# Moving four Q blocks behind the K/V loop, a minimum from GpSimd to VectorE, LN2 statistics from VectorE to ScalarE, and new PSUM banks in a fused attention and FFN kernel

## The chip, the cores and the metric

The kernel runs on one core of one Trainium2 chip. The metric is device time in microseconds (us), the median of several executions. The profile of the core shows a matrix engine (PE), VectorE (DVE), ScalarE (ACT), GpSimd (POOL) and a queue engine (SP) that issues DMAs. In its traces each works through its own list of instructions in order and waits for the others. The program puts its matmuls into eight PSUM banks, 512 columns at most in each, and lets PE use a bank again only when DVE or ACT has read it out.

All runs quoted are marked fast in the record. Two timings of one kernel still differ by up to 0.5% (868.22 to 872.25 us in the runs of before), and part of this document finds out why.

## The reference, cut to what matters

```python
mod = silu(c) @ w_mod                          # six vectors: sa, ca, ga, sb, cb, gb
h = layernorm(x) * (1 + ca) + sa               # x: 2048 tokens x 1024
q, k, v = split(h @ wqkv)                      # 32 heads of 32
pq, pk = phi(q), phi(k)                        # phi(t) = (t > 0 ? t + 1 : exp(t)) + 1e-6
kv = sum over tokens of pk^T v                 # one 32x32 matrix a head
z = sum over tokens of pk
o = (pq @ kv) / (pq . z + 1e-6)
x = x + ga * (o @ wo)
h = layernorm(x) * (1 + cb) + sb               # LN2
x = x + gb * ((gelu(h @ w_gate) * (h @ w_up)) @ w_down)
```

`phi` is computed as min(exp(t), 1) + 1e-6 plus max(t, 0): one ACT pass (exp), one DVE or POOL pass (min), one DVE pass (max and add).

## The kernel before

The tokens are 16 chunks of 128, and four chunks make a token group of 512. The stages are these.

1. **K/V loop.** For each chunk, K and V (four blocks of eight matmuls), `kvacc` (the sum kv, one chunk late), and two Q blocks of the group before. A Q block is eight matmuls of 512 columns for 128 of the 1024 Q columns of one group.
2. **Unit stage.** The Q blocks of the last group, the denominators (`den`), the transposes of kv (`kvt`), eight products kv·Wo (`w2_pair`), and the scaling of pq by 1/den (`bcast`: small matmuls that spread 1/den over the partitions, then DVE multiplications `pqs`).
3. **Wo stage.** Twelve of the sixteen chunks of o·Wo with the residual addition on DVE, LN2 of group 0, the scaling of groups 2 and 3.
4. **FFN** for the four groups, each with `up` and `gate` products and then `down`. The last four Wo chunks lie between products of the first group.

A small scheduler in the program records each operation with what it reads and writes and sets the waits. So the order in the source is the order on each engine. The parts that matter:

```python
def phi(bank, dst_ap, dst_rng, note, min_eng=V):
    ...exp on ACT...
    o = sch.op(min_eng, lambda e: e.tensor_scalar(EB[i], EB[i], 1.0, 1e-6, op0=ALU.min, op1=ALU.add), ...)
    ...max and add on DVE...

def q_evac(sg, qc, b):                       # the last four Q blocks: minimum on POOL
    phi(b, PQ[sg][:, qc, :], ..., G if sg == NSG - 1 and qc >= 4 else V)

for c_ in range(4, NCH):                     # K/V loop
    if c_ % 4 == 0:
        q_todo += [(c_ // 4 - 1, qc) for qc in range(NG)]
    for _ in range(2):
        q_block(*q_todo.pop(0))
    ...K, V, kvacc(c_ - 1), LN1 of chunk c_ + 3...
    if c_ == 13:                             # POOL: iota and four is_equal passes make SEL
        ...
    if c_ >= 12:                             # DVE: Wo *= ga, two rows of blocks a chunk
        ...

# unit stage
q_block(3, 0, False, 0); kvacc(15); zcols(); q_evac(3, 0, 0)
q_block(3, 1, bank=1);   kvbd();    q_block(3, 2, bank=2);  den(0, 5); kvt()
q_block(3, 3, bank=0);   w2_pair(0)
q_block(3, 4, bank=1);   bcast(0, 0); w2_pair(1)
q_block(3, 5, bank=0);   w2_pair(2);  bcast(0, 1); w2_pair(3)
q_block(3, 6, bank=1);   w2_pair(4);  bcast(0, 2); w2_pair(5)
q_block(3, 7, bank=0);   w2_pair(6);  bcast(0, 3); w2_pair(7)

# Wo stage
for c_ in range(12):
    wo_chunk(c_, 2 * (c_ % 2))               # banks 0/1 or 2/3
    if c_ == 1: den(1, 4)
    if 3 <= c_ < 7: bcast(1, c_ - 3)
    if 5 <= c_ < 9: ln2_a(c_ - 5, False)     # statistics on DVE, x-hat on ACT, transpose by DMA
    if c_ == 9: mod2(0, 2)                   # DVE: scale and shift of h
    if c_ == 10: mod2(2, 2)
```

Of the kernel before, what the change touches and what calls it, by code (L numbers as in the profile page):

```python
# [7 lines left out]
ACTF = mybir.ActivationFunctionType  # L8
# [4 lines left out]
D = 1024  # L13
NCH = S // P
NSG = 4
# [201 lines left out]
def bass_adaLN_cond__linear_attn_block__geglu_ffn__prompt_kernel(  # L217
# [14 lines left out]
    with ExitStack() as es:  # L232
# [96 lines left out]
        def r_pq(sg, k0=0, k1=NG, s0=0, s1=SGW):  # L329
            return r_t8(PQO[sg], f"pq{sg}", k0, k1, s0, s1)  # L330
# [240 lines left out]
        KVB = {g: (5 + g // 3, (g % 3) * KV_SLOT) for g in range(NG)}  # L571
        eb_i = [0]

        def phi(bank, dst_ap, dst_rng, note, min_eng=V):
            i = eb_i[0] % 6
            eb_i[0] += 1
            rng = r_2k(EBO[i], f"eb{i}")
            sch.op(A, lambda e: e.activation(EB[i][:, :], PS(bank), ACTF.Exp), prd=pr(bank), wr=rng, note=f"{note}.exp")
            o = sch.op(min_eng, lambda e: e.tensor_scalar(EB[i][:, :], EB[i][:, :], 1.0, 1e-6, op0=ALU.min, op1=ALU.add),
                       rd=rng, wr=rng, deps=[last_g[0]] if min_eng == G else [], note=f"{note}.min")  # L580
            if min_eng == G:
                last_g[0] = o
            sch.op(V, lambda e: e.scalar_tensor_tensor(dst_ap, PS(bank), 0.0, EB[i][:, :], op0=ALU.max, op1=ALU.add),
                   rd=rng, prd=pr(bank), wr=dst_rng, note=f"{note}.add")

# [42 lines left out]
        def q_block(sg, qc, evac=True, bank=None):  # L628
            b = nb() if bank is None else bank
            o = None  # L630
            for dc in range(NDC):
                o = sch.op(T, lambda e, dc=dc: e.matmul(PS(b), WQ[:, dc, qc * P:(qc + 1) * P], H1[sg][:, dc, :],  # L632
                                                        start=(dc == 0), stop=(dc == NDC - 1)),
                           rd=r_w(OFF_WQ, "wq", dc, qc * P, (qc + 1) * P) + r_h1(sg, dc, dc + 1),
                           pwr=(pr(b) if dc == 0 else ()), note=f"q sg{sg} qc{qc} dc{dc}")
            pset_writer(b, o)
            if evac:
                q_evac(sg, qc, b)
            return b

        def q_evac(sg, qc, b):
            phi(b, PQ[sg][:, qc, :], r_pq(sg, qc, qc + 1), f"phiq{sg}.{qc}", G if sg == NSG - 1 and qc >= 4 else V)


        for c_ in range(3):
# [52 lines left out]
        for c_ in range(4, NCH):  # L698
            if c_ % 4 == 0:
                q_todo += [(c_ // 4 - 1, qc) for qc in range(NG)]  # L700
            for _ in range(2):
                q_block(*q_todo.pop(0))
            for jg in range(2):
                b = nb()
                kv_mm(c_, "k", jg, b, list(range(NDC)))
                k_evac(c_, jg, b)
            for jg in range(2):
                b = nb()
                kv_mm(c_, "v", jg, b, list(range(NDC)))
                v_evac(c_, jg, b)  # L710
            if c_ % 2 == 1 and c_ + 2 < NCH:
                mod1(c_ + 1, 2)
            kvacc(c_ - 1)
            if c_ + 3 < NCH:
                ln1(c_ + 3)
                t1d(c_ + 3)
            if c_ == 6:
                o_r = mod_rows(0, 4)
                for k, t in enumerate((6, 7, 8, 9)):
                    wm_dma(t, k)  # L720
                sch.dma(Q, lambda e: e.dma_start(GAB[:, :].rearrange("p (a b) -> p a b", a=2),
                                                 scr_row[0, 0:2, :].rearrange("(o a) b -> o a b", o=1).to_broadcast([P, 2, 512])),
                        wr=R_GAB, deps=[o_r], note="gab")
                sch.dma(Q, lambda e: e.dma_start(GBB[:, :].rearrange("p (a b) -> p a b", a=2),
                                                 scr_row[0, 2:4, :].rearrange("(o a) b -> o a b", o=1).to_broadcast([P, 2, 512])),
                        wr=R_GBB, deps=[o_r], note="gbb")
            if c_ == 9:
                o_r = mod_rows(1, 4)
                sch.dma(Q, lambda e: e.dma_start(SBT[:, :], scr_row[1, 0:2, :].rearrange("a (b p) -> p (a b)", p=P)),
                        wr=r_sm("sbT"), deps=[o_r], note="sbT")  # L730
                sch.dma(Q, lambda e: e.dma_start(CBT[:, :], scr_row[1, 2:4, :].rearrange("a (b p) -> p (a b)", p=P)),
                        wr=r_sm("cbT"), deps=[o_r], note="cbT")
                sch.dma(Q, lambda e: e.dma_start(WO[:], wo_v), wr=[(OFF_WS, OFF_WS + 16384, "wo")], note="wo")
            if c_ == 13:
                gop(lambda e: e.iota(IOTA_B[:].rearrange("p (a b d) -> p a b d", a=NG, b=HPG), [[4, NG], [1, HPG], [0, 32]],
                                     channel_multiplier=-1), wr=R_IOTA2)
                for k in range(4):
                    gop(lambda e, k=k: e.tensor_scalar(SEL[32 * k:32 * (k + 1)].rearrange("p a b -> p (a b)"), IOTA_B[32 * k:32 * (k + 1), :],
                                                       float(-32 * k), None, op0=ALU.is_equal), rd=R_IOTA2, wr=R_SEL)
            if c_ == 11:  # L740
                sch.op(V, lambda e: e.tensor_scalar(CB1T[:, :], CBT[:, :], 1.0, None, op0=ALU.add), rd=r_sm("cbT"), wr=r_sm("cb1T"))
            if c_ >= 12:
                for kc in range((c_ - 12) * 2, (c_ - 12) * 2 + 2):
                    rg = [(OFF_WS + kc * 2048, OFF_WS + (kc + 1) * 2048, "wo")]
                    sch.op(V, lambda e, kc=kc: e.tensor_tensor(WO[:, kc, :], WO[:, kc, :], GAB[:, :], ALU.mult),
                           rd=rg + R_GAB, wr=rg, note=f"wofold {kc}")
        assert not q_todo


        def zcols():  # L750
# [66 lines left out]
            sch.op(V, lambda e: e.tensor_tensor(ap, ap, PS(4 + i).rearrange("p (a b) -> p a b", a=2), ALU.mult),  # L817
                   prd=pr(4 + i), rd=rng, wr=rng, note=f"pqs{pr_}.{r}.{i}")

        q_block(3, 0, False, 0)  # L820
        kvacc(NCH - 1)
        zcols()
        q_evac(3, 0, 0)
        q_block(3, 1, bank=1)
        kvbd()
        q_block(3, 2, bank=2)
        den(0, 5)
        kvt()
        q_block(3, 3, bank=0)
        w2_pair(0)  # L830
        q_block(3, 4, bank=1)
        bcast(0, 0)
        w2_pair(1)
        q_block(3, 5, bank=0)
        w2_pair(2)
        bcast(0, 1)
        w2_pair(3)
        q_block(3, 6, bank=1)
        w2_pair(4)
        bcast(0, 2)  # L840
        w2_pair(5)
        q_block(3, 7, bank=0)
        w2_pair(6)
        bcast(0, 3)
        w2_pair(7)

        wd_q = [0]

# [10 lines left out]
        def wo_chunk(c_, b0):  # L859
# [9 lines left out]
            for half in range(2):  # L869
                pset_writer(b0 + half, last[half])  # L870
            sch.op(V, lambda e: e.tensor_tensor(XALL[:, c_, :], ps_all[:, b0 * 512:(b0 + 2) * 512], XALL[:, c_, :], ALU.add),  # L871
                   prd=pr(b0) + pr(b0 + 1), rd=r_x(c_), wr=r_x(c_), note=f"x1 c{c_}")

        def ln2_a(c_, late):
            ln_stats(c_, "B")
            ln_nm(c_)
            if late:
                i = c_ % 2
                b_, rng = XHD[i], r_2k(OFF_ROW + i * 2048, f"xhd{i}")
            else:  # L880
                b_, rng = xh_buf(c_)
            xhat_act(c_, b_, rng)
            sg, ci = divmod(c_, CPG)
            tdma(Q, H2[sg][:, :, ci * P:(ci + 1) * P], b_[:, :], rng, r_h2(sg, 0, NDC, ci * P, (ci + 1) * P), f"T2 {c_}")
# [3 lines left out]
        for q in (4, 5, 6):  # L888
            wd_dma(q)
        for c_ in range(12):  # L890
            wo_chunk(c_, 2 * (c_ % 2))
            if c_ == 1:
                den(1, 4)
            if 3 <= c_ < 7:
                bcast(1, c_ - 3)
            if 5 <= c_ < 9:
                ln2_a(c_ - 5, False)
            if c_ == 9:
                mod2(0, 2)
            if c_ == 10:  # L900
                mod2(2, 2)
        stream_pair(0, 2)

# [58 lines left out]
        for q in range(4):  # L962
            hook(0, 5 + q, lambda q=q: wd_dma(q))
        for sg in range(NSG):
            for fp in range(NFP):
                if fp + 2 < NFP and not (sg == 0 and fp == 0):
                    stream_pair(sg, fp + 2)
                ffn_fc(sg, 2 * fp)
                ffn_fc(sg, 2 * fp + 1)
                for fn in hooks.get((sg, fp), ()):  # L970
                    fn()
            if sg + 1 < NSG:
                stream_pair(sg + 1, 0)
                stream_pair(sg + 1, 1)
            for ci in range(CPG):
                if sg + 1 < NSG:
                    n0 = (sg + 1) * CPG
                    if ci < 2:
                        ln2_a(n0 + 2 * ci, True)
                        ln2_a(n0 + 2 * ci + 1, True)  # L980
                    else:
                        mod2(n0 + 2 * (ci - 2), 2)
                ffn_down(sg, ci)
# [74 lines left out]
```

## Time and profile before

| | before |
|---|---|
| time, median of 4 runs | 870.47 us (869.93 to 870.85) |
| span of the profiled run | 866.3 us (that run: 868.06 us) |
| PE busy | 832.9 us, 96% of the span |

The first part of the page of before: span, and busy time of the engines with their share.

```profile
span 866.3 us, 11297 instructions
PE 832.9 (96%) x4201; PEld 384.2 (44%) x4281; DVE 500.1 (58%) x896; ACT 288.1 (33%) x469; POOL 43.2 (5%) x65
```

PE is the bottleneck. Only time in which PE idles can be won as long as its work and its pace stay the same. So the list of what PE waits for is the list of what there is to win. Each line of it says: engine, line, tile written, what ended the wait, the total, the number of waits, the longest. Lines of the start of the kernel and those of 0.5 us or less are left out.

```profile
PE ps_all L864 <- DVE xall L871: 1.9, 1, 1.9
PE ps_all L804 <- DVE pq_54 L817: 1.5, 2, 1.2
PE ps_all L918 <- DVE xall L950: 1.4, 1, 1.4
PE ps_all L804 <- DVE pq_55 L817: 1.3, 4, 0.3
PE ps_all L776 <- ACT w_65 L778: 0.7, 1, 0.7
PE ps_all L788 <- DVE kvbd L762: 0.7, 1, 0.7
```

L864 is a Wo chunk that waits for the residual addition in its bank, L804 a `bcast` that waits for the scaling in its banks, L918 the first `up` product of the third FFN group that waits for an output addition, L776 `w2_pair`, L788 `den`. (The start of the kernel has some 15 us more, which the change doesn't touch.)

The timeline of PE in before gives the marks that the rest of this document uses: start, length, line, tiles, and in brackets the idle time ahead of it.

```profile
156.84 0.62 PE L613 MATMUL ps_all<-vs_80,pk_74 128*128 128x129 bf16 x8
189.32 0.62 PE L613 MATMUL ps_all<-vs_80,pk_77 128*128 128x129 bf16 x8
206.18 0.28 PE L804 MATMUL ps_all<-rdhl,sel 32*128 32x256 bf16 x1 [1.20 <-DVE pq_54 L817]
218.39 7.08 PE L864 MATMUL ps_all<-w_65,pq_54 128*128 128x512 bf16 x32 [0.47 <-DVE pq_57 L583]
255.30 11.06 PE L864 MATMUL ps_all<-w_65,pq_56 128*128 128x512 bf16 x47 [1.95 <-DVE xall L871]
266.60 0.38 PE L915 MATMUL ps_all<-h2T_58,wg_90 128*128 128x512 bf16 x1 [0.24 <-DVE h2T_58 L527]
```

The first two are `kvacc` of chunks 11 and 14. They run at the ends of chunks 12 and 15, so between them lie the three chunks that the change thins out. 218.39 is the first Wo chunk and 266.60 the first FFN product.

The timeline of POOL and DVE in before shows the minimum on either engine, and DVE's wait for the one on POOL:

```profile
194.57 0.43 DVE L579 TENSOR_SCALAR eb_101<-eb_101 128x512 f32<-128x512 f32 x1 [0.59 <-ACT eb_101 L578]
202.87 1.94 POOL L579 TENSOR_SCALAR eb_98<-eb_98 128x512 f32<-128x512 f32 x1 [1.37 <-ACT eb_98 L578]
204.84 0.69 DVE L583 SCALAR_TENSOR_TENSOR pq_57<-ps_all,eb_98 128x512 bf16<-128x512 f32 x1 [3.14 <-POOL eb_98 L579]
```

The same operation takes 0.43 us on DVE and 1.94 us on POOL. DVE works in order, so while it waits 3.14 us for POOL the scalings behind it wait too, and behind those PE at 206.18.

### The profile page before, as it was taken

The numbers are of one execution on the slowest core, as the hardware profiler recorded it, in microseconds if no ns is written. First come the engines' busy times: TensorE is split into PE (matmuls) and PEld (weight loads), VectorE is DVE, ScalarE is ACT, GpSimd is POOL, SyncE is SP. The second block draws the span as 40 slices with busy tenths as digits, with TensorE's granted clock in tenths as the row PEclk, the third lists the DMA queues.
The fourth block names the chain that finished last, engine by engine and source line by source line (L and its number), as shares of the span: only waits on it lengthen the run. The fifth ranks groups of instructions, "written<-read, shape, count | busy, mean of one in ns | idle before, by whom it ended". The sixth has DMA issues, their size and how long they took to land.

```text
span 866.3 us, 11297 instructions
## 1 busy us (share of the span) xinstructions
PE 832.9 (96%) x4201; PEld 384.2 (44%) x4281; DVE 500.1 (58%) x896; ACT 288.1 (33%) x469; POOL 43.2 (5%) x65
## 2 busy tenths in 40 slices
PE   3999999998989999999999999999999999999998
PEld 2444444443434444444444444444444444444443
DVE  4467667977686556564355656436655544565522
ACT  4223333335013334531145452024545203445300
POOL 2000000603000000000000001000000100000000
PEclk9999999999999999999999999999999999999999
DMA  9981814002414359442255643135553505555000
GB/s 317 363 230 25 259 34 119 17 1 74 171 25 122 106 160 304 110 120 57 67 151 151 170 110 93 45 110 146 146 150 111 99 25 152 146 146 146 7 19 24
DMA packets 177766, 104.57 MB, mean 121 GB/s; under 512 B 34600, under 2 KB 169768, under 8 KB 177712
## 3 DMA queue, kind: packets, MB, share of 16 engines
q1 hardware_dynamic: 175600, 103.33, 42.2%
q10 hardware_dynamic: 2112, 0.52, 0.6%
q8 instruction: 34, 0.56, 0.3%
q14 instruction: 20, 0.16, 0.1%
HBM read 92.28 MB, written 4.21 MB: 111 GB/s over the span
## 4 chain that ended last, share of the span: by engine, by line
PE 88%; DVE 6%; issue 2%; POOL 1%; ACT 1%; DMA 1%; ACTq 0%; SPq 0%; POOLq 0%; DVEq 0%
PE ps_all L918 23%; PE ps_all L942 22%; PE ps_all L915 21%; PE ps_all L591 10%; PE ps_all L632 6%; PE ps_all L864 4%; DVE st L471 1%; DVE st L470 1%; POOL rs L475 1%; PE ps_all L613 1%; DVE xall L871 1%; PE ps_all L561 0%; PE ps_all L545 0%; DMA h2T_58<-xh_104 0%; DMA xall<-in_A_x_dram 0%
## 5 line engine op out<-in xcount | busy, mean ns | idle before, releaser
L926 ACT ACTIVATE q_0_109<-ps_all 128x512 f32<-128x512 f32 x56 | 33.4, 597 | 169.2 <-PE ps_all L915 161.5
L948 DVE TENSOR_TENSOR ps_all<-ps_all,gbb 128x512 f32<-128x512 f32 x32 | 22.4, 698 | 95.7 <-PE ps_all L942 95.7
L928 DVE SCALAR_TENSOR_TENSOR ww_111<-q_0_109,ps_all 128x512 f32<-128x512 f32 x56 | 38.5, 687 | 56.1 <-ACT guh_96 L927 56.1
L931 DVE SCALAR_TENSOR_TENSOR ww_111<-th_113,guh_96 128x512 f32<-128x512 f32 x56 | 38.8, 693 | 39.0 <-ACT th_113 L930 39.0
L931 DVE SCALAR_TENSOR_TENSOR ww_112<-th_114,guh_97 128x512 f32<-128x512 f32 x56 | 38.8, 692 | 38.9 <-ACT th_114 L930 38.9
L928 DVE SCALAR_TENSOR_TENSOR ww_112<-q_1_110,ps_all 128x512 f32<-128x512 f32 x56 | 38.5, 688 | 36.5 <-ACT guh_97 L927 36.5
L926 ACT ACTIVATE q_1_110<-ps_all 128x512 f32<-128x512 f32 x56 | 33.4, 597 | 54.9 <-PE ps_all L915 52.9
L930 ACT ACTIVATE th_114<-ww_112 128x512 f32<-128x512 f32 x56 | 35.2, 629 | 42.2 <-DVE ww_112 L928 42.2
L930 ACT ACTIVATE th_113<-ww_111 128x512 f32<-128x512 f32 x56 | 35.2, 629 | 42.2 <-DVE ww_111 L928 42.2
L475 POOL TENSOR_TENSOR rs<-ve,neghalf 128x1 f32<-128x1 f32 x32 | 17.6, 551 | 592.6 <-DVE ve L473 584.4
L933 DVE TENSOR_TENSOR yT<-ww_112,ps_all 128x512 bf16<-128x512 f32 x56 | 38.5, 687 | 1.9
L933 DVE TENSOR_TENSOR yT<-ww_111,ps_all 128x512 bf16<-128x512 f32 x56 | 38.4, 686 | 1.9
L927 ACT ACTIVATE guh_97<-ps_all 128x512 f32<-128x512 f32 x56 | 33.1, 592 | 0.0
L927 ACT ACTIVATE guh_96<-ps_all 128x512 f32<-128x512 f32 x56 | 33.1, 591 | 0.0
L942 PE MATMUL ps_all<-wd_66,yT 128*128 128x512 bf16 x128 | 32.9, 379 | 0.0
L942 PE MATMUL ps_all<-wd_70,yT 128*128 128x512 bf16 x128 | 32.8, 379 | 0.0
L942 PE MATMUL ps_all<-wd_72,yT 128*128 128x512 bf16 x124 | 32.6, 379 | 0.2
L942 PE MATMUL ps_all<-wd_69,yT 128*128 128x512 bf16 x124 | 32.6, 379 | 0.2
L942 PE MATMUL ps_all<-wd_68,yT 128*128 128x512 bf16 x125 | 32.4, 379 | 0.2
L942 PE MATMUL ps_all<-wd_67,yT 128*128 128x512 bf16 x125 | 32.2, 379 | 0.2
L942 PE MATMUL ps_all<-wd_71,yT 128*128 128x512 bf16 x124 | 32.0, 379 | 0.2
L918 PE MATMUL ps_all<-h2T_60,wu_93 128*128 128x512 bf16 x80 | 30.3, 379 | 1.4 <-DVE xall L950 1.4
(288 smaller groups left out, 1683.3 us busy)
## 6 DMA issues: line engine op xcount, KB each, us to landing
wg_90<-in_B_w_gate_dram SPq DMA_DIRECT2D x20, 512.0 KB, 3.8
wu_93<-in_B_w_up_dram SPq DMA_DIRECT2D x20, 512.0 KB, 5.0
wg_91<-in_B_w_gate_dram SPq DMA_DIRECT2D x20, 512.0 KB, 3.9
wu_94<-in_B_w_up_dram SPq DMA_DIRECT2D x20, 512.0 KB, 5.1
wg_92<-in_B_w_gate_dram SPq DMA_DIRECT2D x16, 512.0 KB, 3.8
wu_95<-in_B_w_up_dram SPq DMA_DIRECT2D x16, 512.0 KB, 5.1
out_dram<-xall SPq DMA_DIRECT2D x32, 128.0 KB, 1.7
wmst_81<-in_w_mod_dram SPq DMA_DIRECT2D x3, 1024.0 KB, 7.4
```

The lines of the kernel that those rows point to most:

```text
L591: o = sch.op(T, lambda e, dc=dc: e.matmul(PS(bank), H1[sg][:, dc, ci * P:(ci + 1) * P], W_[:, dc, jg * 512:(jg + 1) * 512], start=(dc == 0 ...
L632: o = sch.op(T, lambda e, dc=dc: e.matmul(PS(b), WQ[:, dc, qc * P:(qc + 1) * P], H1[sg][:, dc, :], start=(dc == 0), stop=(dc == NDC - 1)), ...
L864: last[half] = sch.op(T, lambda e, g=g, half=half: e.matmul(PS(b0 + half), PQ[sg][:, g, ci * P:(ci + 1) * P], W2[:, g, half * 512:(half + ...
L915: og = sch.op(T, lambda e, dc=dc: e.matmul(PS(bg), WG[slot][:, dc, e_ * P:(e_ + 1) * P], H2[sg][:, dc, :], start=(dc == 0), stop=(dc == ND ...
L918: ou = sch.op(T, lambda e, dc=dc: e.matmul(PS(bu), WU[slot][:, dc, e_ * P:(e_ + 1) * P], H2[sg][:, dc, :], start=(dc == 0), stop=(dc == ND ...
L926: sch.op(A, lambda e: e.activation(Q1[j][:, :], PS(bg), ACTF.Square, scale=math.sqrt(GELU_A)), prd=pr(bg), wr=rq, note=f"q1 {fc}")
L927: ogh = sch.op(A, lambda e: e.activation(GUH[j][:, :], PS(bg), ACTF.Copy, scale=0.5), prd=pr(bg), wr=rg, note=f"gh {fc}")
L928: sch.op(V, lambda e: e.scalar_tensor_tensor(WW[j][:, :], Q1[j][:, :], 1.0, PS(bg), op0=ALU.add, op1=ALU.mult), rd=rq, prd=pr(bg), wr=rw, ...
L930: sch.op(A, lambda e: e.activation(TH[j][:, :], WW[j][:, :], ACTF.Tanh, scale=GELU_C), rd=rw, wr=rt, note=f"th {fc}")
L931: sch.op(V, lambda e: e.scalar_tensor_tensor(WW[j][:, :], TH[j][:, :], 1.0, GUH[j][:, :], op0=ALU.add, op1=ALU.mult), rd=rt + rg, wr=rw, n ...
L933: sch.op(V, lambda e: e.tensor_tensor(YT[:, fc, :], WW[j][:, :], PS(bu), ALU.mult), rd=rw, prd=pr(bu), wr=r_yt(fc), note=f"yT {fc}")
L942: o = sch.op(T, lambda e, b=b, fc=fc, half=half: e.matmul(PS(b), YT[:, fc, ci * P:(ci + 1) * P], WDT[fc // 4][:, fc % 4, half * 512:(half ...
```

## The change

The intent: PE is always busy in chunks 13 to 15 (31.70 of the 31.86 us from 157.46 to 189.32) and idles in the unit stage (23.34 of the 28.49 us from 189.90 to 218.39 are busy). So four Q blocks of the third group (number 2) go from those chunks into the unit stage. The LN2 statistics of the first 512 tokens go to ACT, which has little to do in the Wo stage (5.61 of 48.21 us busy in before). PSUM banks are dealt anew, among them the bank pairs of the FFN, which start afresh at each group. The minimum that ran on POOL goes back to DVE.

```diff
-        def phi(bank, dst_ap, dst_rng, note, min_eng=V):
+        def phi(bank, dst_ap, dst_rng, note):             # the minimum always on DVE
...
-            for _ in range(2):
+            for _ in range({13: 1, 14: 1, 15: 0}.get(c_, 2)):
                 q_block(*q_todo.pop(0))
...
+        first_q = q_next(False)                            # the unit stage: 12 Q blocks
         kvacc(NCH - 1)
         zcols()
+        q_evac(*first_q)
+        q_next()
+        den(0, 3)                                          # was bank 5, after kvbd
         kvbd()
+        q_next()
+        q_next()
         kvt()
+        for u in range(NG):
+            q_next()
+            w2_pair(u)                                     # banks 2/3, as before
+            if u in (0, 2, 4, 5):
+                bcast(0, (0, 2, 4, 5).index(u))
...
+        def ln2_stats_act(c_, b_, rng):
+            ...ACT: Identity with accum_out (sum); POOL: -sum/D
+            ...ACT: Square with bias -mean and accum_out; POOL: var+eps, pow(-0.5), -mean*rstd
...
         for c_ in range(12):
-            wo_chunk(c_, 2 * (c_ % 2))
-            if c_ == 1:
+            wo_chunk(c_, 2 * ((c_ + 1) % 2))
+            if c_ == 0:
                 den(1, 4)
-            if 3 <= c_ < 7:
-                bcast(1, c_ - 3)
-            if 5 <= c_ < 9:
-                ln2_a(c_ - 5, False)
+            if c_ in (2, 3, 5, 6):
+                bcast(1, (2, 3, 5, 6).index(c_))
+            if c_ < 4:
+                ln2_a(c_, False)                           # with ln2_stats_act
             if c_ == 9:
                 mod2(0, 2)
-            if c_ == 10:
                 mod2(2, 2)
...
         for sg in range(NSG):
+            gu_i[0] = 1 if sg == 0 else 0                  # FFN bank pairs start afresh
```

More of the change, by code (lines that the diff above doesn't have):

```diff
@@ L578, in phi @@
             sch.op(A, lambda e: e.activation(EB[i][:, :], PS(bank), ACTF.Exp), prd=pr(bank), wr=rng, note=f"{note}.exp")
-            o = sch.op(min_eng, lambda e: e.tensor_scalar(EB[i][:, :], EB[i][:, :], 1.0, 1e-6, op0=ALU.min, op1=ALU.add),
-                       rd=rng, wr=rng, deps=[last_g[0]] if min_eng == G else [], note=f"{note}.min")
-            if min_eng == G:
-                last_g[0] = o
+            sch.op(V, lambda e: e.tensor_scalar(EB[i][:, :], EB[i][:, :], 1.0, 1e-6, op0=ALU.min, op1=ALU.add),
+                   rd=rng, wr=rng, note=f"{note}.min")
             sch.op(V, lambda e: e.scalar_tensor_tensor(dst_ap, PS(bank), 0.0, EB[i][:, :], op0=ALU.max, op1=ALU.add),
@@ L641, in q_evac @@
         def q_evac(sg, qc, b):
-            phi(b, PQ[sg][:, qc, :], r_pq(sg, qc, qc + 1), f"phiq{sg}.{qc}", G if sg == NSG - 1 and qc >= 4 else V)
+            phi(b, PQ[sg][:, qc, :], r_pq(sg, qc, qc + 1), f"phiq{sg}.{qc}")
         for c_ in range(3):
@@ L746, in bass_adaLN_cond__linear_attn_block__geglu_ffn__prompt_kernel @@
                            rd=rg + R_GAB, wr=rg, note=f"wofold {kc}")
-        assert not q_todo
         def zcols():
@@ L818, in pq_scale, with q_next @@
                    prd=pr(4 + i), rd=rng, wr=rng, note=f"pqs{pr_}.{r}.{i}")
-        q_block(3, 0, False, 0)
+        q_todo += [(NSG - 1, qc) for qc in range(NG)]
+        qn = [0]
+        def q_next(evac=True):
+            sg, qc = q_todo.pop(0)
+            b = (0, 1, 2, 0)[qn[0]] if qn[0] < 4 else (qn[0] + 1) % 2
+            qn[0] += 1
+            q_block(sg, qc, evac, b)
+            return sg, qc, b
+        first_q = q_next(False)
         kvacc(NCH - 1)
         zcols()
-        q_evac(3, 0, 0)
-        q_block(3, 1, bank=1)
+        q_evac(*first_q)
+        q_next()
+        den(0, 3)
         kvbd()
-        q_block(3, 2, bank=2)
-        den(0, 5)
+        q_next()
+        q_next()
         kvt()
-        q_block(3, 3, bank=0)
-        w2_pair(0)
-        q_block(3, 4, bank=1)
-        bcast(0, 0)
-        w2_pair(1)
-        q_block(3, 5, bank=0)
-        w2_pair(2)
-        bcast(0, 1)
-        w2_pair(3)
-        q_block(3, 6, bank=1)
-        w2_pair(4)
-        bcast(0, 2)
-        w2_pair(5)
-        q_block(3, 7, bank=0)
-        w2_pair(6)
-        bcast(0, 3)
-        w2_pair(7)
+        for u in range(NG):
[3 more added lines that the diff above has]
+                bcast(0, (0, 2, 4, 5).index(u))
+        assert not q_todo
         wd_q = [0]
@@ L872, in wo_chunk @@
                    prd=pr(b0) + pr(b0 + 1), rd=r_x(c_), wr=r_x(c_), note=f"x1 c{c_}")
+        def ln2_stats_act(c_, b_, rng):
+            src = XALL[:, c_, :]
+            sm, sq = STA[:, c_, 0:1], STA[:, c_, 1:2]
+            rst, rmv = r_smc("st", c_, 48), r_smc("mv", c_, 8)
+            sch.op(A, lambda e: e.activation(b_[:, :], src, ACTF.Identity, accum_out=sm), rd=r_x(c_), wr=rng + rst, note=f"sum B{c_}")
+            gop(lambda e: e.tensor_scalar(MVA[:, c_, 0:1], sm, -1.0 / D, None, op0=ALU.mult), rd=rst, wr=rmv, note=f"nmean B{c_}")
+            sch.op(A, lambda e: e.activation(b_[:, :], src, ACTF.Square, bias=MVA[:, c_, 0:1], accum_out=sq),
+                   rd=r_x(c_) + rmv, wr=rng + rst, note=f"sq B{c_}")
+            gop(lambda e: e.tensor_scalar(VEA[:, c_:c_ + 1], sq, 1.0 / D, 1e-5, op0=ALU.mult, op1=ALU.add), rd=rst, wr=r_smc("ve", c_, 4), note=f"ve B{c_}")
+            gop(lambda e: e.tensor_tensor(RSA[:, c_:c_ + 1], VEA[:, c_:c_ + 1], NEGHALF[:, :], ALU.pow),
+                rd=r_smc("ve", c_, 4) + r_sm("neghalf"), wr=r_smc("rs", c_, 4), note=f"rstd B{c_}")
+            gop(lambda e: e.tensor_tensor(NMA[:, c_:c_ + 1], MVA[:, c_, 0:1], RSA[:, c_:c_ + 1], ALU.mult),
+                rd=rmv + r_smc("rs", c_, 4), wr=r_smc("nm", c_, 4), note=f"nm {c_}")
         def ln2_a(c_, late):
-            ln_stats(c_, "B")
-            ln_nm(c_)
+            if late:
+                ln_stats(c_, "B")
+                ln_nm(c_)
             if late:
@@ L881, in ln2_a @@
                 b_, rng = xh_buf(c_)
+                ln2_stats_act(c_, b_, rng)
             xhat_act(c_, b_, rng)
```

## The prediction

> **What bounds the kernel.** TensorE: the page gives it 832.9 of 866.3 us busy; a 512-column matmul takes 0.216 us (16 in 3.46 us, chain of waits) at clock 1.00. The change removes no matmul, so I ask only where PE idles and which idle it fills.
>
> **Where PE idles (timeline, PE only).** From the end of kvacc 14 (189.9 us) to the first FFN matmul (266.6 us) are 76.7 us. The work in it, at measured paces: 8 Q blocks 13.8, kvacc 0.45, two den 2.0, eight kvT 0.55, W2 3.5, eight bcast 4.4, twelve Wo chunks 41.5, about 66.1. So 10.5 us are lost:
> - 189.9 to 218.4 (Q of group 3, W2, first scaling): 28.5 us for 21.4 of work, 7.1 lost. PE waits for kvbd, for the scaling's banks (206 to 208, 215 to 218), for W2 copies. The Q minimum on POOL takes 1.92 us against 0.43 on DVE; DVE, in order, waits 3.14 and 2.65 us for it, the scalings behind it.
> - 218.4 to 266.6 (Wo): 48.2 us for 44.7 of work, 3.5 lost. DVE is the cause: statistics cost 0.6+0.7+0.2+0.15+0.16 us a chunk plus a POOL wait of 0.7, so a Wo chunk waits 1.95 us for its bank, and the FFN waits for the last h2T modulation.
> The list of waits also shows one 1.4 us wait of the FFN for the output evacuation (bank 4/5) at the start of the third group.
>
> **What the change does.**
> 1. Four Q blocks (6.9 us of PE) leave chunks 13 to 15, where PE is over 99% busy, and fill gaps after. Nearly the whole 6.9 us should come off before kvacc 14. DVE is 9.86 of 10 us busy at 160 to 180, since building SEL on POOL (11.7 us) stretches its minimum from 0.43 to 1.09-1.25 us[...]. I allow 0.2-0.5 us of wait for h1T of chunk 14.
> 2. After: 12 Q blocks, 28.3 us of work. Stepping through the queues I find waits of 0.9 us for kvT (the reciprocal, 1.75 us, is now ahead of kvbd on DVE), 1.4 us at the fourth bcast (units 4 and 5 are adjacent: DVE 3.6 us against PE 2.7), and 1.6 us for the last W2 copy, because Wo chunk 0 now uses the W2 banks 2/3. Wo starts about 215.5 instead of 218.4: 2.9 us won.
> 3. In the Wo stage four statistics (7.3 us) leave DVE. On ACT a pass of 1024 costs about 1.1-1.25 us (xhat 1.24 in the trace[...]). Three passes and four POOL steps make 6.5-7 us a chunk in series, 26-28 us for four: ready about when chunk 9 asks, with 1-3 us to spare. Most of the 3.5 us should go: 3.2 won.
> 4. Restarting the bank pairs per FFN group removes the 1.4 us wait.
>
> Sum: 2.9 + 3.2 + 1.4 = 7.5 us. Predicted 863.2 us, range 860.3 to 866.8. Chances: faster by over 2% 0.02, within 2% 0.97, slower 0.01.
>
> **What would show each step.** PE: kvacc 14 ends near 183; Wo chunk 0 starts near 215.5; FFN starts near 260.4. No POOL minimum. No PE wait of Wo for the residual addition; DVE busy in the Wo stage down by 7 us, ACT up by 9-10. The third FFN group starts without wait.
>
> **What would make it wrong.** The ACT/POOL chain longer than 7 us a chunk, so that DVE stalls before the modulation at chunk 9 and delays the FFN; DVE saturation at chunks 13-14 turning the removed Q work into waits; more DVE lag than I step through in the unit loop[...].

The 6.5-7 us a chunk behind the 3.2 us were the author's estimate; the trace of before has ACT passes of 1024 elements at 1.01 to 1.24 us. That POOL stretches DVE's minimum is in that trace: 0.53 to 1.25 us during POOL's passes for SEL (158.97 to 170.71), 0.41 to 0.43 us after them (173.56 to 187.19). Why is not shown.

## The result

| | before | after |
|---|---|---|
| time, median of 4 runs | 870.47 us | 861.35 us (861.06 to 861.72) |
| ratio after/before | | 0.9896, 95% interval 0.9879 to 0.9913 |
| span of the profiled run | 866.3 us | 859.6 us |
| kvacc 11 to kvacc 14 (chunks 13 to 15) | 32.48 us | 26.92 us |
| kvacc 14 to the first Wo chunk (unit stage) | 29.07 us | 32.32 us |
| first Wo chunk to the FFN (Wo stage) | 48.21 us | 45.16 us |
| FFN to the end | 599.70 us | 598.11 us |

A ratio is the mean time of one kernel's fast runs over that of the other's of the same rounds, so it is not quite the ratio of the medians. The last four rows are differences of marks in the timelines, as shown for before.

The page of after:

```profile
span 859.6 us, 11395 instructions
PE 837.6 (97%) x4281; PEld 384.1 (45%) x4281; DVE 494.9 (58%) x880; ACT 297.0 (35%) x485; POOL 37.9 (4%) x73
```

PE's busy time is no clue here. It went up by 4.7 us, but the first trace has 80 matmul records fewer (4201 against 4281, with 4281 weight loads in both), so the two sums don't compare. DVE lost 5.2 us and ACT gained 8.9.

What PE waits for in after (lines of the start and one of 0.4 us left out):

```profile
PE ps_all L589 <- DVE h1T L527: 2.2, 4, 0.7
PE ps_all L861 <- ACT w L775: 1.2, 1, 1.2
PE ps_all L801 <- DVE pq L814: 0.6, 2, 0.3
```

The waits for the residual addition (1.9 us) and for the output addition (1.4 us) are gone. `bcast` waits 0.6 us in place of 2.8. Two have come: for h1T in the K loop (1.3 of the 2.2 us belong to the start of the kernel, the rest is new) and for the last W2 copy (L775). The marks in the timeline of PE in after:

```profile
157.09 0.62 PE L611 MATMUL ps_all<-vs,pk 128*128 128x129 bf16 x8
168.39 0.59 PE L589 MATMUL ps_all<-wk,h1T 128*128 128x512 bf16 x2
169.28 1.16 PE L589 MATMUL ps_all<-wk,h1T 128*128 128x512 bf16 x4 [0.30 <-DVE h1T L527]
171.03 2.33 PE L589 MATMUL ps_all<-wk,h1T 128*128 128x512 bf16 x10 [0.58 <-DVE h1T L527]
184.01 0.62 PE L611 MATMUL ps_all<-vs,pk 128*128 128x129 bf16 x8
216.33 3.63 PE L861 MATMUL ps_all<-w,pq 128*128 128x512 bf16 x16 [1.23 <-ACT w L775]
261.49 0.38 PE L927 MATMUL ps_all<-h2T,wg 128*128 128x512 bf16 x1
```

The first line is `kvacc` of chunk 11. The next three are K of chunk 14, which PE has to start and stop for because the scale and shift of h1T come late. The timeline of DVE in after shows why: the eight small passes took 3.81 us.

```profile
167.23 3.81 DVE L527 TENSOR_SCALAR h1T<-h1T,ca1T,saT 128x256 bf16<-128x256 bf16 x8
```

Two things are left to explain. The time fell by 9.1 us but the profile by 6.7. And it is not plain which part of the change did what.

### The profile page after: what moved, and what is told of

Same layout as the page of the kernel before. It is cut to its first block, busy times and chain, and to the rows that moved or that the text cites. A ratio compares the mean times of both kernels' runs of the same rounds, so it can differ in the third digit from the quotient of the medians.

```text
span 859.6 us, 11395 instructions
## 1 busy us (share of the span) xinstructions
PE 837.6 (97%) x4281; PEld 384.1 (45%) x4281; DVE 494.9 (58%) x880; ACT 297.0 (35%) x485; POOL 37.9 (4%) x73
## 4 chain that ended last, share of the span: by engine, by line
PE 93%; DVE 4%; issue 1%; ACT 1%; POOL 0%; DMA 0%; SPq 0%; ACTq 0%; DVEq 0%; POOLq 0%
PE ps_all L927 22%; PE ps_all L954 22%; PE ps_all L930 22%; PE ps_all L589 11%; PE ps_all L861 7%; PE ps_all L630 6%; DVE eb L579 1%; PE ps_all L611 1%; DVE h1T L527 1%; DVE st L471 0%; PE ps_all L801 0%; DVE st L470 0%; PE ps_all L561 0%; PE ps_all L545 0%; POOL rs L475 0%
## 5 line engine op out<-in xcount | busy, mean ns | idle before, releaser
L927 PE MATMUL ps_all<-h2T,wg 128*128 128x512 bf16 x896 | 339.9, 379 | 0.0
L930 PE MATMUL ps_all<-h2T,wu 128*128 128x512 bf16 x896 | 339.7, 379 | 0.0
L954 PE MATMUL ps_all<-wd,yT 128*128 128x512 bf16 x896 | 194.0, 379 | 0.0
L927 PEld LDWEIGHTS ps_all<-h2T,wg 128*128 128x128 bf16 x896 | 87.5, 98 | 106.0 <-issue 0.2
L954 PEld LDWEIGHTS ps_all<-wd,yT 128*128 128x128 bf16 x896 | 87.5, 98 | 105.9
L930 PEld LDWEIGHTS ps_all<-h2T,wu 128*128 128x128 bf16 x896 | 87.6, 98 | 105.7
L940 DVE SCALAR_TENSOR_TENSOR ww<-q,ps_all 128x512 f32<-128x512 f32 x112 | 77.0, 688 | 92.4 <-ACT guh L939 92.4
L943 DVE SCALAR_TENSOR_TENSOR ww<-th,guh 128x512 f32<-128x512 f32 x112 | 77.6, 693 | 77.9 <-ACT th L942 77.9
L942 ACT ACTIVATE th<-ww 128x512 f32<-128x512 f32 x112 | 70.4, 629 | 84.4 <-DVE ww L940 84.4
L945 DVE TENSOR_TENSOR yT<-ww,ps_all 128x512 bf16<-128x512 f32 x112 | 76.9, 687 | 3.8
```

Source lines behind the costliest of these rows:

```text
L927: og = sch.op(T, lambda e, dc=dc: e.matmul(PS(bg), WG[slot][:, dc, e_ * P:(e_ + 1) * P], H2[sg][:, dc, :], start=(dc == 0), stop=(dc == ND ...
L930: ou = sch.op(T, lambda e, dc=dc: e.matmul(PS(bu), WU[slot][:, dc, e_ * P:(e_ + 1) * P], H2[sg][:, dc, :], start=(dc == 0), stop=(dc == ND ...
L940: sch.op(V, lambda e: e.scalar_tensor_tensor(WW[j][:, :], Q1[j][:, :], 1.0, PS(bg), op0=ALU.add, op1=ALU.mult), rd=rq, prd=pr(bg), wr=rw, ...
L942: sch.op(A, lambda e: e.activation(TH[j][:, :], WW[j][:, :], ACTF.Tanh, scale=GELU_C), rd=rw, wr=rt, note=f"th {fc}")
L943: sch.op(V, lambda e: e.scalar_tensor_tensor(WW[j][:, :], TH[j][:, :], 1.0, GUH[j][:, :], op0=ALU.add, op1=ALU.mult), rd=rt + rg, wr=rw, n ...
L945: sch.op(V, lambda e: e.tensor_tensor(YT[:, fc, :], WW[j][:, :], PS(bu), ALU.mult), rd=rw, prd=pr(bu), wr=r_yt(fc), note=f"yT {fc}")
```

## The experiments

Twelve kernels ran, all correct. In all profiles the same marks were read. Times are medians; "ratio" is to the runs of before in the same call (e1 to e4, e5 to e7 with e10, and e8, e9, e11, e12 are three calls, each on another chip). The stage columns come from one profile of each kernel.

| run | time us | ratio (95%) | kvacc 11 to 14 | unit stage | Wo stage | FFN to end |
|---|---|---|---|---|---|---|
| e1_before_again | 870.82 | 1.0001 (0.9987 to 1.0015) | 32.48 | 30.64 | 48.23 | 599.71 |
| e2_ffn_banks_only | 869.11 | 0.9982 (0.9970 to 0.9994) | 32.47 | 30.53 | 48.24 | 598.08 |
| e3_q_move_only | 866.07 | 0.9954 (0.9943 to 0.9966) | 26.92 | 32.60 | 48.21 | 599.73 |
| e4_wo_stage_only | 866.33 | 0.9954 (0.9942 to 0.9966) | 32.48 | 30.42 | 45.16 | 599.65 |
| e5_min_on_dve | 865.06 | 0.9945 (0.9930 to 0.9960) | 32.48 | 25.98 | 48.18 | 599.67 |
| after | 861.35 | 0.9896 (0.9879 to 0.9913) | 26.92 | 32.32 | 45.16 | 598.11 |
| e6_stats_on_dve | 864.52 | 0.9938 (0.9924 to 0.9952) | 26.93 | 32.31 | 48.46 | 598.12 |
| e7_sel_spread | 860.42 | 0.9889 (0.9870 to 0.9907) | 25.53 | 32.32 | 45.16 | 598.16 |
| e8_w2_tail | 860.54 | 0.9888 (0.9875 to 0.9900) | 26.92 | 30.93 | 45.15 | 598.15 |
| e9_both | 859.14 | 0.9876 (0.9863 to 0.9889) | 25.54 | 30.92 | 45.15 | 598.08 |
| e11_no_q_move | 860.49 | 0.9892 (0.9879 to 0.9905) | 32.48 | 25.99 | 45.15 | 598.11 |
| e10_before_filled | 870.06 | 0.9997 (0.9982 to 1.0013) | 32.47 | 29.07 | 48.97 | 599.67 |
| e12_wo_stage_filled | 864.89 | 0.9946 (0.9934 to 0.9958) | 32.47 | 29.09 | 46.84 | 599.63 |

A stage that a kernel doesn't change repeats to 0.1 us from profile to profile, except where the clock dips (below): from the FFN to the end, the seven profiles with the FFN banks of before lie between 599.63 and 599.73 us. So the stage columns tell apart what the intervals of the times don't.

### e1_before_again: the kernel before as its own control

No edit.

> The kernel before, unchanged, as a control. The change gained 9.1 us in the timed runs, but its profile is only 6.7 us shorter than the profile of before (859.6 against 866.3 us), and the profiled run of before took 868.06 us where its three timed runs took 869.93 to 870.85. Theory: the first profile of before fell some 2 us short of that kernel's usual time; then this run's profile has a span of about 868.7 us and shows where the 2 us lie. Rival: profiles are as long as timed runs and the change gains 2 us in something that the profiles don't show; then the span is 866.3 again while the time is 870.5. Ratio to before: 1.000 within 0.001.

The profiled run took 870.76 us with a span of 869.0. So the theory holds: the first profile of before was a fast run of that kernel. The start was 1.1 us later (it varies from run to run: `kvacc` of chunk 11 stands at 156.84 us in the first profile of before, at 157.94 us here), and the unit stage took 30.64 us in place of 29.07. The stretches of 2 us around 206 to 214 us in this profile show why. The columns are the stretch, its length, busy time and instructions of PE, weight loads, DVE, ACT and POOL, then the granted PE clock, the DMA share and GB/s.

```profile
206.00:208.00 2.00, 0.50 (x3) 0.18 (x2) 2.00 (x4) 1.28 (x2) 1.49 (x1) 1.00 0.61 182
208.00:210.00 2.00, 1.36 (x15) 0.52 (x14) 1.68 (x4) 0.00 (x0) 0.43 (x1) 0.74 0.00 0
210.00:212.00 2.00, 1.67 (x5) 0.72 (x6) 2.00 (x4) 0.89 (x1) 0.00 (x0) 0.50 0.00 0
212.00:214.00 2.00, 2.00 (x13) 0.76 (x14) 0.42 (x1) 0.52 (x2) 0.00 (x0) 0.90 0.75 221
```

PE was busy for 0.50 of the 2 us from 206 us, and waited 0.32 us three times more up to 209.07. Then its clock fell to 0.50 and came back. The clock missing in the last three stretches, (0.26 + 0.50 + 0.10) x 2 us, is 1.72 us, which would be a half clock for 3.4 us (an estimate from this sum). The other dips in the stretches that were read, summed in the same way, give 1.70 to 1.72 us too: one later dip each in e4, e10 and e12, and one near 32 us in before, after, e3, e4, e8, e9, e11 and e12. A Q block at 210.87 us took 2.48 us, from its start to that of the next product, in place of 1.73:

```profile
207.28 0.28 PE L804 MATMUL ps_all<-rdhl,sel 32*128 32x256 bf16 x1 [1.18 <-DVE pq L817]
210.87 2.65 PE L632 MATMUL ps_all<-h1T,wq 128*128 128x512 bf16 x8
213.35 0.59 PE L776 MATMUL ps_all<-wo,kvt 128*128 128x512 bf16 x2
```

The single waits of PE ahead of the dip were 1.18 us and less (1.18 us, then three of 0.32 us). In the first profile of before the same stretches all show 1.00, although PE waited 1.20 us there too (at 206.18). What sets the dip off this pair of profiles does not show.

This can be checked over all runs of before. Of 37 executions (31 that ran beside the experiments for comparison, and the six of e1), 3 had a mean clock of 0.999 or 1.000 and took 868.22 to 868.53 us. The 34 others had 0.991 to 0.996 and took 869.00 to 872.25 us, mean 870.35. The two groups don't overlap and lie 2.0 us apart. The first profile of before (868.06 us, 0.998), which is not among the 37, goes with the short ones. All four executions of after had 0.998 or 0.999. So about 2 us of the 9.1 are the clock: before loses it in most runs (34 of 37), after in none of its four.

### e2_ffn_banks_only: the FFN bank pairs alone

```diff
         for sg in range(NSG):
+            gu_i[0] = 0
             for fp in range(NFP):
```

> Before, with only the PSUM bank pairs of the FFN restarted at each token group. Theory: this alone takes away the 1.4 us wait at the start of the third group, so 869.0 us (ratio 0.9984), and the wait for the output evacuation is gone from the list of PE waits. Rival: the next wait takes its place (for the h2T modulation), so under 0.5 us gained.

From the FFN to the end took 598.08 us in place of 599.71, so 1.6 us are gained, and the ratio agrees (0.9982 of 870.4 us is 1.6 us). The wait for the output addition is gone from the list. The theory holds.

### e3_q_move_only: the Q blocks and the minimum alone

The edit: after, with the Wo stage, `ln2_a` and the FFN banks of before put back.

> After, with the Wo stage, the LN2 statistics and the FFN banks of before put back: only the four moved Q blocks and the Q minimum on DVE remain. Theory (parts add up): the first Wo chunk starts 2.1 us earlier, as in the two profiles, and the Wo stage then lasts 48.2 us as before; so 868.4 us (ratio 0.9976). Rival: the Wo stage of before was limited by its own DVE chain, which starts earlier too but has more backlog: less than 1 us gained. If the timed gain is larger, 4 us or more, the first profile of before flattered this part.

The gain is 4.0 us, and the last sentence of the expectation applies: the first profile of before, without the clock dip, made this part look small. Against e1, from kvacc 11 to Wo it is 59.52 us in place of 63.12, so 3.6 us. The Wo stage is exactly as long as before (48.21 us). The marks in the timeline of PE in e3:

```profile
156.84 0.62 PE L611 MATMUL ps_all<-vs,pk 128*128 128x129 bf16 x8
216.36 7.08 PE L861 MATMUL ps_all<-w,pq 128*128 128x512 bf16 x31 [1.51 <-DVE pq L581]
```

But this run holds two edits at once: the minimum on DVE in place of POOL, and the four moved Q blocks with what comes with them in the unit stage (`den` ahead of `kvbd`, other places of `bcast`, other banks). Hence e5. The second edit was not taken apart further; "the Q move" below means all of it.

### e4_wo_stage_only: the Wo stage alone

The edit: before, with `ln2_stats_act`, the new `ln2_a` and the new order of the Wo stage, on the banks of before.

> Before, with only the Wo stage changed: LN2 statistics of the first 512 tokens on ACT, LN2 right after its Wo chunk, and the new places of den, bcast and the modulation; banks as before. Theory: the Wo stage goes from 48.2 to 45.2 us, so 867.5 us (ratio 0.9965), and no PE wait for the residual addition is left. Rival: part of it comes from the earlier Q stage, so less than 2 us.

The Wo stage took 45.16 us, to 0.01 us what it takes in after, and the wait for the residual addition is gone. So the 3.07 us of this stage belong to this part and don't depend on the rest. The timed ratio gives 4.0 us with an interval of about 1 us either way, so it includes the 3.07.

### e5_min_on_dve: only the minimum moves from POOL to DVE

```diff
-            phi(b, PQ[sg][:, qc, :], ..., f"phiq{sg}.{qc}", G if sg == NSG - 1 and qc >= 4 else V)
+            phi(b, PQ[sg][:, qc, :], ..., f"phiq{sg}.{qc}")
```

> Before, with only the Q minimum of the last four blocks taken from POOL and given to DVE (0.43 us in place of 1.92). No Q block is moved. Theory: moving the Q blocks is what fills PE's idle time, the place of the minimum is second; then the stage from kvacc 14 to the first Wo chunk falls from 30.6 us by about 1 us, and the time by about 1 us (ratio 0.9988), against 4.0 us for the Q move that contains it. Rival: POOL's minimum alone made the loss; then 3 us or more are gained here (ratio 0.9965 or less) and the half-rate clock stretch near 208 us is gone too.

The rival won, and clearly: 865.06 us, ratio 0.9945, 4.8 us gained with no Q block moved. The unit stage fell from 30.64 to 25.98 us (from 29.07 in the first profile of before, which has no clock dip: 3.1 us). All five executions had a mean clock of 0.998. The marks in the timeline of PE in e5, and two of its waits:

```profile
156.39 0.62 PE L613 MATMUL ps_all<-vs,pk 128*128 128x129 bf16 x8
188.87 0.62 PE L613 MATMUL ps_all<-vs,pk 128*128 128x129 bf16 x8
205.28 0.28 PE L804 MATMUL ps_all<-rdhl,sel 32*128 32x256 bf16 x1 [0.32 <-DVE pq L817]
214.85 3.40 PE L864 MATMUL ps_all<-w,pq 128*128 128x512 bf16 x15
PE ps_all L776 <- ACT w L778: 1.2, 2, 0.7
PE ps_all L788 <- DVE kvbd L762: 0.7, 1, 0.7
```

The `bcast` wait of 1.2 us is gone, and the first Wo chunk starts without a wait. From kvacc 11 to Wo it is 32.48 + 25.98 = 58.46 us here and 59.52 us in e3, which has the same minimum and the moved Q blocks on top. So the Q move lost more than it filled; by these stages it cost 1.1 us. (The timed ratios, 0.9945 and 0.9954, point the same way, with intervals that overlap.) It did fill idle time: the two waits shown for e5, 1.9 us together, are not in the list of after. What it cost can be seen in after too: K of chunk 14 is held up by 1.4 us (26.92 us against 32.48 less four Q blocks of 1.73 us, which would be 25.56), and the last W2 copy is waited for.

### e11_no_q_move: after without the moved Q blocks

The edit: before with the edits of e2, e4 and e5 together.

> After without the moved Q blocks: the order of before up to the first Wo chunk with the Q minimum on DVE (e5_min_on_dve), the new Wo stage (e4_wo_stage_only) and the restarted FFN banks (e2_ffn_banks_only). Theory, new since e5: moving the Q blocks gains nothing by itself and costs about 0.8 us (h1T of chunk 14 1.4 us, the last W2 copy 1.2 us, against waits it fills); so kvacc 11 to Wo 58.5 us against 59.2 and 860.5 us, 0.5 to 1.0 us faster than after (ratio 0.9888). Rival, as in the prediction: the moved Q blocks fill idle time; then this is 2 us or more slower than after (863.4, ratio 0.992).

The marks in its timeline of PE:

```profile
156.67 0.62 PE L613 MATMUL ps_all<-vs,pk 128*128 128x129 bf16 x8
215.14 3.62 PE L864 MATMUL ps_all<-w,pq 128*128 128x512 bf16 x16
```

From kvacc 11 to Wo 58.47 us against 59.24 in after, so 0.8 us shorter in the profile. The time is 860.49 us, and the ratio 0.9892 against 0.9896: the intervals overlap, so the timed runs show only that it isn't slower than after. The prediction's reading would have made it 2 us slower or more, and that is excluded. The parts add up: from kvacc 11 to the end, e1 to e11 is 9.33 us, and the same stages of e5, e4 and e2, each measured alone, give 4.66, 3.07 and 1.63, which is 9.36. From e1 to after it is 8.55 us. That is 4.66 (minimum; 1.7 of it is the clock dip that e1's profile has and e5's hasn't) less 0.78 (Q move and its banks) plus 3.07 (Wo stage) plus 1.60 (FFN banks).

### e6_stats_on_dve: the LN2 statistics back on DVE

```diff
         def ln2_a(c_, late):
-            if late:
-                ln_stats(c_, "B")
-                ln_nm(c_)
+            ln_stats(c_, "B")
+            ln_nm(c_)
...
                 b_, rng = xh_buf(c_)
-                ln2_stats_act(c_, b_, rng)
```

> After, with the LN2 statistics of the first 512 tokens back on DVE at the same places of the order (right after Wo chunks 0 to 3). Theory: the statistics had to leave DVE; with 7.3 us more there PE waits again for the residual addition and for the scaling, some 2 us in the Wo stage (45.2 to 47 us), time 863.4 us (ratio to before 0.992). Rival: starting LN2 four chunks earlier was what mattered, and DVE, busy 29.5 of 45.2 us, has room: the Wo stage stays at 45.2 us and the time at 861.3 (ratio 0.9896).

The Wo stage is 48.46 us, so the whole gain of the stage is gone, more than the 2 us that I expected. The wait for the residual addition is back, at another place:

```profile
243.60 3.63 PE L861 MATMUL ps_all<-w,pq 128*128 128x512 bf16 x16 [1.66 <-DVE xall L868]
```

The new order alone gains nothing; it needs the statistics off DVE. (Statistics on ACT in the old order were not tried.)

### e7_sel_spread: SEL built in four pieces

SEL is the matrix of ones that `bcast` uses. POOL builds it in about 12.9 us (iota and four passes) after chunk 12. The edit, on after:

```diff
-            if c_ == 13:
+            if c_ == 10:
                 gop(lambda e: e.iota(IOTA_B[:]...))
-                for k in range(4):
+            if 10 <= c_ < 14:
+                for k in (c_ - 10,):
                     gop(lambda e, k=k: e.tensor_scalar(SEL[32 * k:32 * (k + 1)]..., op0=ALU.is_equal), ...)
```

In `ln_stats` the POOL operation is also entered as the last one on POOL, so that the pieces wait for it.

> After, with the SEL matrix built by POOL in four pieces after chunks 10 to 13 instead of in one stretch of 11.7 us after chunk 12. Theory: the 1.4 us that PE waits for h1T of chunk 14 in the profile of after come from POOL's hold on DVE (the modulation there took 3.81 us, elsewhere 2.13); spread out, DVE's slack of chunks 10 to 12 takes it, the stretch from kvacc 11 to kvacc 14 falls from 26.9 to about 25.6 us, and the time to 860.0 us (ratio 0.988). Rival: DVE is simply short of time in chunks 13 and 14 whatever POOL does, or the pieces make new waits in chunks 10 to 12: under 0.5 us gained.

From kvacc 11 to 14 it is 25.53 us, so the 1.4 us are gone. The timeline of DVE in this run has the passes over h1T of chunk 14 at their length of elsewhere:

```profile
166.97 2.13 DVE L527 TENSOR_SCALAR h1T<-h1T,ca1T,saT 128x256 bf16<-128x256 bf16 x8
```

So the wait came from POOL holding DVE up, as the theory said: the passes took 3.81 us beside POOL's passes for SEL and 2.13 us without (POOL's last piece ended at 164.98 here). DVE by itself has time enough. The time is 860.42 us, 0.9 below after, but the ratio's interval overlaps that of after.

### e8_w2_tail and e9_both

```diff
-        def w2_pair(g):
-            b0 = 2
+        def w2_pair(g, b0=2):
...
         for u in range(NG):
+            if u == NG - 1:
+                w2_pair(u, 4)               # banks 4/5, ahead of the last Q block
             q_next()
-            w2_pair(u)
+            if u < NG - 1:
+                w2_pair(u)
```

> After, with the last W2 product issued ahead of the last Q block and into banks 4/5, so that both of its copies run while PE does that Q block. Theory: the 1.2 us that the first Wo chunk waits for the last W2 copy go away; from kvacc 14 to Wo 31.0 us in place of 32.3, time 860.1 us (ratio 0.9882). Rival: the first Wo chunk then waits for the scaling of the last heads instead; under 0.5 us.

The unit stage is 30.93 us in place of 32.32, and the wait for the W2 copy is gone from the list. The theory holds in the stage; the time, 860.54 us, is 0.4 us short of the expectation.

> After, with SEL built in four pieces (e7_sel_spread) and the last W2 product moved (e8_w2_tail). If the two add up: from kvacc 11 to the FFN 101.8 us in place of 104.4, time 858.8 us (ratio 0.987). If the one wait hides behind the other: 860.0.

The two add up: from kvacc 11 to the FFN 101.61 us (expected 101.8). The time is 859.14 us, ratio 0.9876, the fastest version, 11 us faster than before and 2 us faster than after (2.8 us by the stages; the intervals of the two ratios still overlap). The marks in its timeline:

```profile
213.57 3.62 PE L864 MATMUL ps_all<-w,pq 128*128 128x512 bf16 x16
258.72 0.38 PE L930 MATMUL ps_all<-h2T,wg 128*128 128x512 bf16 x1
```

With both repairs the Q move pays at last: from kvacc 11 to Wo 56.46 us against 58.47 without it (e11). The 2.0 us are about what e11 still waits for `kvbd` (0.7 us) and for W2 copies (1.2 us), and e9 has neither wait. (e11 doesn't hold the two repairs, and e11 with them was not run. For SEL there was no wait left in it to repair, and it had no wait for the last W2 copy at the first Wo chunk.)

### e10_before_filled and e12_wo_stage_filled: more work for PE, to keep the clock up

```diff
-        def w2_pair(g):
+        def w2_pair(g, reps=1):
             b0 = 2
-            for half in range(2):
+            for half in [h for _ in range(reps) for h in range(2)]:
...
-        w2_pair(2)
+        w2_pair(2, 4)
         bcast(0, 1)
```

e10 is this edit on before, e12 the same on e4. Each repeat overwrites the bank with the same values.

> Before, with the two matmuls of the third W2 product issued four times over into the same two banks (same result, 1.3 us more PE work), just ahead of the broadcast for which PE waits 1.2 us. Theory: in most runs of before PE's clock falls to half for about 3 us near 208 us because PE idles there (the profiles of three runs show 0.50 in a slice of 2 us, the first profile of before doesn't); keeping PE busy over the wait keeps the clock up, so the stage from kvacc 14 to Wo falls from 30.6 to about 29.1 us and the time by 1.3 to 1.6 us although work was added (ratio 0.998). Rival: the clock dip has another cause; then the time is unchanged or up by as much as 1 us and the dip stays.

The unit stage fell from 30.64 to 29.07 us with 1.3 us of work added, and near 208 us the clock stays at 1.00. But the time didn't change. The stretches of this profile show a dip elsewhere:

```profile
206.00:208.00 2.00, 1.06 (x12) 0.42 (x15) 2.00 (x4) 1.02 (x1) 1.19 (x1) 1.00 0.02 5
208.00:210.00 2.00, 2.00 (x21) 0.96 (x14) 2.00 (x4) 0.97 (x1) 0.00 (x0) 1.00 0.00 0
254.00:256.00 2.00, 0.83 (x3) 0.38 (x4) 1.97 (x3) 1.24 (x1) 0.00 (x0) 0.83 0.00 0
256.00:258.00 2.00, 2.00 (x6) 0.64 (x5) 1.27 (x5) 0.27 (x1) 0.55 (x1) 0.50 0.68 131
258.00:260.00 2.00, 2.00 (x9) 0.89 (x8) 1.97 (x3) 0.97 (x1) 0.00 (x0) 0.81 0.00 0
```

The wait ahead of it, from the timeline of PE:

```profile
255.17 7.04 PE L864 MATMUL ps_all<-w,pq 128*128 128x512 bf16 x24 [1.95 <-DVE xall L871]
```

PE waited 1.95 us for the residual addition up to 255.17, and the half clock follows right after. So neither theory was right as a whole: the dip left the place of the filler and came at the next long wait. But a wait alone doesn't make a dip: the profiles of before, e1 and e5 hold the same wait of 1.9 us, e3 has 1.94 us of idle PE between 250 and 254 us, and in the stretches read after it, up to 260 us, the clock is 1.00 in all four.

> e4_wo_stage_only with the third W2 product issued four times over as in e10. In e10 the half-rate stretch near 208 us was gone from the profile but one stood near 256 us instead, right behind the 1.9 us wait for the residual addition; here that wait is gone as well. Theory: PE's idle stretches set off the half clock; then no half-rate stretch is left but that of the start, every run has a mean clock of 0.998 or more, and the time is 864.9 us (ratio 0.9938) although 1.3 us of PE work were added. Rival: the stretch comes anyway, elsewhere, and the clock stays at 0.995 to 0.996: 866.3 us.

Here the runs split. Four of six executions had a mean clock of 0.998 and took 864.54 to 864.95 us, as the theory says. Two had 0.995 and took 867.43 and 867.73 us. The profile fell on one of the two, and its dip, 0.50 from 220 to 222 us, follows a stretch of `bcast` waits of 0.32 us each and one of 0.47 us at the first Wo chunk. Without the filler, e4 had one run of five at 0.999 (865.42 us) and four at 0.995 (866.04 to 867.50 us). With the filler four runs of six were undisturbed, without it one of five; that is too few runs to call the dip rarer. It came here after short waits alone. The four dips outside of the start that the stretches show (e1, e4, e10, e12) all come on idle PE: after the waits given above in e1, e10 and e12, and in e4, where the clock is 0.90 from 206 to 208 us, with PE busy for only 1.13 of the 2 us from 204 and 0.94 of the 2 us from 206. That idle PE sets off the half clock fits these four; it was not shown, since equal waits in other profiles bring no dip.

## Why the prediction was right or wrong

The total was right: predicted 863.2 us with a range from 860.3 to 866.8, measured 861.35. The mechanism named for one of the two large parts, the unit stage, was wrong. That the total came so close is in part luck: the steps were put 0.8 us too high by the profiles (7.5 for 6.7), and the 2 us of the clock, which the prediction didn't know of, lay on the other side.

- **"Four Q blocks leave chunks 13 to 15 and fill gaps after. Nearly the whole 6.9 us should come off before kvacc 14."** 5.6 us came off (32.48 to 26.92). The wait for h1T of chunk 14 was 1.4 us, not "0.2-0.5". The prediction gives the stretch by POOL for the minimum only; the eight passes over h1T took 3.81 us instead of 2.13 to 2.65. e7 shows the cause. The minimum was stretched in after as well: 1.25 us instead of 0.43 (at 162.43), while POOL's four passes for SEL, about 2.8 us each, ran from 159.22 to 170.89.
- **"Wo starts about 215.5 instead of 218.4: 2.9 us won."** It started at 216.33, 2.1 us earlier than in the first profile. Against e1, from kvacc 11 to Wo, the gain is 3.9 us. The step that failed is the attribution: I had noted that the minimum on POOL holds DVE up by 3.14 and 2.65 us, yet credited the win to the moved Q blocks. e5 shows 3.1 us from the minimum alone against the first profile, and 4.7 us against e1 with its clock dip. By the stages after is longer than e11 and e3 longer than e5, so the Q move cost 0.8 to 1.1 us as built.
- **The waits that I found by stepping through the queues** (kvT 0.9, fourth `bcast` 1.4, last W2 copy 1.6 us) are all there, and smaller: kvT about 0.4 (an estimate from PE's timeline: the eight transposes stretch from 193.00 to 193.91, and in before's chain of waits they take 0.55 us), `bcast` 0.6, W2 copy 1.2. e8 confirms the last by removing it.
- **Wo stage, "3.2 won".** 3.05 in the profile. DVE's part in it is right: e6 puts the statistics back and loses it all. ACT's chain of three passes and four POOL steps took 5.34 and 5.65 us for the second and third chunk (which began at 228.90 and 234.14), not the estimated "6.5-7". The first took 7.75 us (from 221.25), since POOL had the steps after `den` ahead of it. All four took 23.8 us, not "26-28", so the chain had room to spare. The passes of 1024 elements took 1.04 us without a pointer operand, 1.15 us with the bias and 1.24 us with bias and scale. Each of the two with an accumulator output has a second instruction in the trace, ACTIVATION_READ_ACCUMULATOR, of 0.18 to 0.19 us.
- **FFN banks, "removes the 1.4 us wait".** 1.6 us, shown alone by e2.
- **Not in the prediction: the clock.** Before loses some 2 us of clock in 34 of the 37 control runs, by their mean clock (0.991 to 0.996); the profile of one of them, e1, shows it as a stretch down to 0.50. The profile that I read was one of the few without it, although its own page said 868.06 us beside three timings of 869.93 to 870.85. That gap of 2 us was in plain view and I didn't ask about it. It is why the measured gain (9.1 us) is larger than the sum of the steps (7.5 us).

## What to carry to other kernels

When a change has several parts, take the smallest one alone first: here one operation on the wrong engine was worth more in its stage than the whole rearrangement around it, because DVE, working in order, waited up to 3.14 us in before for the 1.9 us minimum on POOL and held up the scalings behind it. When work is moved into idle time, look at what the thinned stage was hiding: PE was busy throughout chunks 13 to 15 because the Q blocks covered DVE's lateness, and 1.4 us of it came to light without them (the waits for h1T of chunk 14). Compare the time of the profiled run with the timed runs before reading the profile; where they differ by more than the runs among themselves, take the profile again.
